# Where the q-k products of chunks 2 to 5 stand among the feed-forward products

## The chip, the cores and the metric

The kernel runs on one core of a Trainium2 chip. The metric is the time of one execution on the device in microseconds (us). Before the change it is 245.2 us, the median of 5 runs (244.85 to 246.48). The engines of a core work side by side, each through its own list of instructions in order: TensorE (PE, matrix products; PEld are its weight loads), VectorE (DVE), ScalarE (ACT), GpSimd (POOL) and SyncE (SP, which here only starts transfers).

## The reference

Two parts follow each other: a retention layer with a running state, and a feed-forward layer on its result.

```python
# q, k, v: 4 batches x 8 heads x 768 positions x 64
for t in range(S):
    state = gamma * state + einsum('bhd,bhe->bhde', k[:, :, t], v[:, :, t])
    y[:, :, t] = scale * einsum('bhd,bhde->bhe', q[:, :, t], state)
# x: y as 3072 rows of 512
xn = x / sqrt(mean(x * x) + 1e-6) * rms_g
out = (silu(xn @ w_gate) * (xn @ w_val)) @ w_out      # 512 -> 1536 -> 512
```

`gamma` is a constant of the head, between 1 - 1/32 and 1 - 1/4096.

## The kernel before, in words

**Chunks and batches.** The 768 positions are cut into 6 chunks of 128 rows (`NCH`, line 35). A chunk holds 4 batches of 128 rows, so 512 rows (`GT`, line 41) go through the feed-forward layer together. Within a chunk the retention is computed as a masked product of q and k, and what came before is added through the state.

**The pieces of one batch of one chunk** (chunks 2 to 5):
- `cast` (line 186): POOL turns q and k into bfloat16 and multiplies v by its decay; SP then starts a transposing transfer each for q and k (line 200), which gives `qT` and `kT`.
- `piece_a` (line 222), "A": 8 products of k and q on PE, 64 rows deep, one for each head, into two PSUM tiles `a_ps0` and `a_ps1` (line 228). DVE multiplies each of them by the causal mask into `am`, two instructions of 128x512 (line 234).
- `piece_y` (line 237), "Y": 8 products `am` by v (line 246), 4 products of q by the state (line 251), and, except in the last chunk, 4 products of k and v for the new state (line 257). DVE then scales the result into `x` (line 261), ACT squares and sums it (`xsq`, line 265), POOL makes `ms` (line 286) and `rstd` (line 289) of the sum, DVE adds the new state to `st_f` (line 273), and POOL casts it to `st_b` (line 282).
- `piece_n` (line 292), "N": DVE multiplies `x` by `rstd` and by `g_bc`, the norm's weights (line 297), and SP starts the transposing transfer that puts the batch's columns into `xnT` (line 299), the input of the feed-forward products of that chunk. `g_bc` is loaded once, by SP (line 456).
- `piece_x` (line 304) does no work for these chunks: it drops the batch's entry from a table.

The four batches share a PSUM pool of 4 tiles for `a_ps`, `y_ps` and `kv_ps` (`aps`, line 49). An A takes two of them, a Y two (one in the last chunk).

**The feed-forward layer of one chunk** is a list of 16 slots (`ffn`, line 337). Slots 0 to 11 ("gv") make one block of 128 hidden units each: 4 products for the gate, 4 for the value (line 351), a SiLU of the gate on ACT (`sg`, line 354), and on DVE the product of `sg` and the value (`hT`, line 355). Slots 12 to 15 ("down") make the output of one batch each: 12 products, the n-th of which needs block n of `hT` (line 386), a copy by ACT (`o_sb`, line 391) and a transfer out by SP (line 392). The gate, value and output products take their PSUM tiles from a second pool of 4 (`fps`, line 50).

**The order of the work** is written out by hand: the kernel runs under a manual schedule (line 31), and what a slot issues stands on each engine in the order in which it was issued. The main loop (line 426) goes through the slots of chunk c's feed-forward layer and, after each slot, issues those pieces of chunk c + 1 that a plan assigns to that slot. A plan gives for each piece four slot numbers, one per batch (`PLAN` for chunks 2 to 5, `PLAN1` for chunk 1; lines 320 and 322). Within one slot the pieces come batch by batch, and within a batch in the order cast, t, a, y, n, x (line 328). In slot 13 the pieces come ahead of the slot's own products (line 433). The loads of q, k and v of chunk c + 2 are issued by SP in the slots 5, 7, 9 and 11, ahead of the pieces of those slots (line 444).

In what follows, **pass c** is the stretch from the first gate product of chunk c to the first of chunk c + 1. The passes 1 to 4 carry the pieces of the chunks 2 to 5, so these four hold all that `PLAN` orders. Pass 0 follows `PLAN1`, and pass 5 has no pieces.

Of the kernel before, what the change touches and what calls it, by code (L numbers as in the profile page):

```python
# [17 lines left out]
def kernel(  # L18
# [297 lines left out]
    def begin(c):  # L316
        cur[c, "xnT"] = work.tile([128, KS, GT], BF16, name="xnT", bufs=2)


    PLAN = dict(cast=(0, 1, 2, 3), t=(1, 3, 5, 7), a=(4, 6, 8, 10), y=(6, 8, 10, 12), n=(8, 10, 12, 13), x=(8, 10, 12, 14))  # L320

    PLAN1 = dict(cast=(4, 6, 8, 11), t=(8, 10, 12, 15), a=(9, 11, 14, 17), y=(10, 13, 16, 19), n=(12, 15, 18, 21), x=(13, 17, 20, 22))

    def attention(c):
        s = [[] for _ in range(24 if c == 1 else 16)]
        s[0].append(lambda: begin(c))
        plan = PLAN1 if c == 1 else PLAN
        pieces = dict(cast=cast, t=piece_t, a=piece_a, y=piece_y, n=piece_n, x=piece_x)
# [156 lines left out]
```

## Time and profile before

| | before |
|---|---|
| median of 5 runs | 245.2 us |
| the profiled execution: its own time | 244.82 us |
| span of its trace, first to last instruction | 243.1 us |
| PE busy | 223.2 us (92%) |
| DVE busy | 128.9 us (53%) |
| POOL busy | 96.2 us (40%) |
| ACT busy | 86.4 us (36%) |
| share of the chain that ended last | PE 79%, DMA 7%, DVE 5%, POOL 3% |

How to read it: a profile is one execution of the program, recorded instruction by instruction. The busy times show how much each engine did, but not what bounded the time. For that there is a chain, followed back from the last instruction: at each step to the instruction that released it, or to the one before it on its engine. A row of the timeline gives the start, the duration, the engine, the line, the tile written and the tiles read, how many instructions are merged in the row, and in brackets the idle time before it and who ended it. Matrix products are pipelined: each is recorded as 0.38 us long, but in a full stream one starts 0.216 us after the other. Likewise DVE instructions recorded as 0.68 us start 0.60 us apart.

### The profile page before, as it was taken

To read this page: it belongs to the slowest core of one execution; us is meant where nothing else is said; L and a number is where in the kernel's file an instruction comes from. 1 tells how busy PE (TensorE), PEld (TensorE's weight loads), DVE (VectorE), ACT (ScalarE), POOL (GpSimd) and SP (SyncE) were. 2 spreads that over 40 slices of the span, in tenths; PEclk is the share of its full clock that TensorE was granted. 3 is DMA by queue.
4 is the path that set the end of the run, shared out by engine and by line. 5 is a ranking of instruction groups with operands and counts; after the bars stand their busy time and mean duration, and the time that the engine had idled before them with its cause. 6 is when DMAs were issued, how large, how long until landed. Compare 5 with 4: busy or idle time off the path is not lost.

```text
span 243.1 us, 4161 instructions
## 1 busy us (share of the span) xinstructions
PE 223.2 (92%) x1534; PEld 115.8 (48%) x1559; DVE 128.9 (53%) x214; ACT 86.4 (36%) x164; POOL 96.2 (40%) x178
## 2 busy tenths in 40 slices
PE   1779999999599989899999999999999999999993
PEld 0546744465245545344555445555445454444443
DVE  6587435777237596035896046895137772234300
ACT  7463334533232243132243222333233433233221
POOL 8977245674733235930224940244920211000000
PEclk9998999999999999999999999999999999999999
DMA  8999999989999799954999454999553114200022
GB/s 137 176 193 206 205 223 199 185 121 226 203 175 276 159 197 211 259 122 96 231 183 198 127 128 80 212 219 199 162 101 65 22 24 115 102 0 3 0 86 88
DMA packets 107157, 35.94 MB, mean 148 GB/s; under 512 B 99008, under 2 KB 103872, under 8 KB 107136
## 3 DMA queue, kind: packets, MB, share of 16 engines
q1 hardware_dynamic: 95232, 29.24, 59.5%
q0 software_dynamic: 11232, 6.29, 19.1%
q8 instruction: 12, 0.20, 0.4%
q10 hardware_dynamic: 672, 0.13, 0.3%
q14 instruction: 9, 0.07, 0.1%
HBM read 28.58 MB, written 6.29 MB: 143 GB/s over the span
## 4 chain that ended last, share of the span: by engine, by line
PE 79%; DMA 7%; DVE 5%; POOL 3%; issue 2%; ACT 1%; SPq 0%; DVEq 0%; POOLq 0%; ACTq 0%
PE g_ps L351 24%; PE v_ps L351 24%; PE o_ps L386 21%; DMA v_f<-in_v_dram 5%; PE a_ps L228 2%; PE y_ps L246 2%; DMA g_bc<-in_moe_rms_g_dram 2%; DVE am L234 2%; PE y_ps L251 1%; PE kv_ps L257 1%; DVE xn L301 1%; PE o_ps L376 1%; PE xt_ps L311 1%; POOL qb L78 1%; DVE x L261 1%
## 5 line engine op out<-in xcount | busy, mean ns | idle before, releaser
L355 DVE TENSOR_TENSOR hT<-sg,v_ps 128x512 bf16<-128x512 bf16 (+1 forms) x73 | 49.5, 679 | 79.4 <-PE v_ps L351 75.0
L351 PE MATMUL g_ps<-xnT,wg_b 128*128 128x512 bf16 (+2 forms) x294 | 73.3, 368 | 1.8 <-ACT o_sb L391 1.1
L351 PE MATMUL v_ps<-xnT,wv_b 128*128 128x512 bf16 (+2 forms) x296 | 73.2, 367 | 0.4
L354 ACT ACTIVATE sg<-g_ps 128x512 bf16<-128x512 f32 (+1 forms) x73 | 42.8, 588 | 61.3 <-PE g_ps L351 59.6
L386 PE MATMUL o_ps<-wo_b,hT 128*128 128x512 bf16 x269 | 61.7, 379 | 0.4 <-issue 0.2
L351 PEld LDWEIGHTS <-wv_b 128*128 128x128 bf16 x304 | 29.1, 98 | 33.1
L351 PEld LDWEIGHTS <-wg_b 128*128 128x128 bf16 x304 | 27.4, 98 | 32.1 <-DMA xnT<-xn 1.5
L386 PEld LDWEIGHTS <-hT 128*128 128x128 bf16 x276 | 26.3, 98 | 29.6
L286 POOL TENSOR_SCALAR ms<-ssq 128x1 f32<-128x1 f32 x24 | 4.5, 189 | 80.5 <-ACT xsq L265 80.1
L391 ACT COPY o_sb<-o_ps 128x512 f32<-128x512 f32 x23 | 13.4, 584 | 39.5 <-PE o_ps L386 37.5
L265 ACT ACTIVATE xsq<-x 128x512 f32<-128x512 f32 x20 | 12.6, 630 | 38.3 <-DVE x L261 38.3
L234 DVE TENSOR_TENSOR am<-a_ps,causal 128x512 bf16<-128x512 f32 x40 | 25.6, 682 | 0.0
L193 POOL TENSOR_TENSOR vp<-v_f,vdec 128x512 bf16<-128x512 f32 x20 | 20.7, 1037 | 2.8 <-DMA v_f<-in_v_dram 2.8
L191 POOL CAST qb<-q_f 128x512 bf16<-128x512 f32 x20 | 12.1, 607 | 14.1 <-DMA q_f<-in_q_dram 13.8
L282 POOL CAST st_b<-st_f 64x256 bf16<-64x256 f32 x40 | 17.1, 427 | 1.3
L297 DVE SCALAR_TENSOR_TENSOR xn<-x,rstd,g_bc 128x512 bf16<-128x512 f32 x16 | 12.6, 788 | 7.2 <-POOL rstd L289 5.6
L261 DVE TENSOR_TENSOR x<-y_ps,ydec 128x512 f32<-128x512 f32 x20 | 13.7, 686 | 3.5 <-PE y_ps L251 3.5
L192 POOL CAST kb<-k_f 128x512 bf16<-128x512 f32 x20 | 12.2, 609 | 5.3 <-DMA k_f<-in_k_dram 5.3
L289 POOL TENSOR_TENSOR rstd<-ms,mhalf 128x1 f32<-128x1 f32 x24 | 13.2, 551 | 2.0
L246 PE MATMUL y_ps<-vp,am 128*128 128x64 bf16 x192 | 10.9, 199 | 2.5 <-DVE am L234 2.4
L246 PEld LDWEIGHTS <-am 128*128 128x128 bf16 x192 | 9.3, 102 | 8.1 <-DVE am L234 3.7
L273 DVE TENSOR_TENSOR st_f<-st_f,kv_ps 128x512 f32<-128x512 f32 x16 | 10.8, 678 | 0.0
(68 smaller groups left out, 134.6 us busy)
## 6 DMA issues: line engine op xcount, KB each, us to landing
out_dram<-o_sb SPq DMA_DIRECT2D x23, 256.0 KB, 2.2
q_f<-in_q_dram SPq DMA_DIRECT2D x21, 256.0 KB, 4.6
k_f<-in_k_dram SPq DMA_DIRECT2D x21, 256.0 KB, 5.1
v_f<-in_v_dram SPq DMA_DIRECT2D x21, 256.0 KB, 5.0
wo_b<-in_moe_w_out_dram POOLq DMA_DIRECT2D x3, 512.0 KB, 5.9
v_f<-in_v_dram POOLq DMA_DIRECT2D x3, 256.0 KB, 5.4
wg_b<-in_moe_w_gate_dram POOLq DMA_DIRECT2D x2, 384.0 KB, 7.6
wv_b<-in_moe_w_val_dram POOLq DMA_DIRECT2D x2, 384.0 KB, 8.5
```

The costliest lines, as they stand in the source:

```text
L193: nc.gpsimd.tensor_tensor(out=vp, in0=v_f, in1=vdec[:, c, :, None].to_broadcast([128, H, D]), op=ALU.mult)
L234: nc.vector.tensor_tensor(out=am[:, i], in0=a_ps[i], in1=mask, op=ALU.mult)
L246: nc.tensor.matmul(y_ps[:, h, :], d["am"][:, i, hp, :], d["vp"][:, h, :], start=first, stop=last, skip_group_check=True)
L261: nc.vector.tensor_tensor(out=x, in0=y_ps, in1=ydec[:, c, :, None].to_broadcast([128, H, D]), op=ALU.mult)
L265: nc.scalar.activation(xsq, x.rearrange("p h d -> p (h d)"), AF.Square, accum_out=ssq)
L282: nc.gpsimd.tensor_copy(st_b[b][r, :, i * 64:i * 64 + 64], st_f[b][r, :, i * 64:i * 64 + 64])
L289: nc.gpsimd.tensor_tensor(out=rstd, in0=ms, in1=mhalf, op=ALU.pow)
L351: nc.tensor.matmul(ps[:, n - n0, :], w_b[:, s, n * 128:(n + 1) * 128], xnT[:, s, t], start=s == 0, stop=s == KS - 1)
L354: nc.scalar.activation(sg, g_ps, AF.Silu)
L355: nc.vector.tensor_tensor(out=hT[:, n0:n1, t], in0=sg, in1=v_ps, op=ALU.mult)
L386: nc.tensor.matmul(o_ps, hT[:, n, b * C:(b + 1) * C], wo_b[:, n, :], start=n == 0, stop=n == NFF - 1)
L391: nc.scalar.copy(o_sb, o_ps)
```

## The change

One line changes, the plan for the chunks 2 to 5. The four numbers are the slots of the batches 0 to 3.

```diff
-    PLAN = dict(cast=(0, 1, 2, 3), t=(1, 3, 5, 7), a=(4, 6, 8, 10), y=(6, 8, 10, 12), n=(8, 10, 12, 13), x=(8, 10, 12, 14))
+    PLAN = dict(cast=(0, 1, 2, 3), t=(1, 3, 5, 7), a=(6, 6, 10, 10), y=(8, 9, 12, 12), n=(10, 11, 13, 13), x=(10, 11, 13, 14))
```

The same in a table (A0 is `piece_a` of batch 0, and so on; the pieces stand in the order of issue):

| slot | pieces before | pieces after |
|---|---|---|
| 4 | A0 | |
| 6 | Y0 A1 | A0 A1 |
| 8 | N0 Y1 A2 | Y0 |
| 9 | | Y1 |
| 10 | N1 Y2 A3 | N0 A2 A3 |
| 11 | | N1 |
| 12 | N2 Y3 | Y2 Y3 |
| 13 | N3 | N2 N3 |

No instruction is added or taken away. The casts, the loads, the feed-forward slots, the pools and the numbers of their buffers stay as they are.

## The prediction

> **What bounds the kernel now.** I read the page's engine line and chain first, then the stretches of the five passes, then PE's waits, and last the timelines around one pair of pieces.
>
> The chain of the page is mostly PE. The stretches (start:end; length, then busy time and instruction count of PE, PEld, DVE, ACT, POOL; clock; DMA share; GB/s) are the passes 1 to 4:
>
> ```profile
> PE 79%; DMA 7%; DVE 5%; POOL 3%; issue 2%; ACT 1%; SPq 0%; DVEq 0%; POOLq 0%; ACTq 0%
> ```
> ```profile
> 64.48:102.44 37.96, 35.81 (x237) 17.58 (x241) 20.61 (x32) 12.53 (x25) 17.36 (x32) 1.00 1.02 208
> 102.44:137.98 35.54, 35.33 (x237) 17.63 (x241) 20.59 (x32) 11.47 (x23) 13.54 (x27) 1.00 0.82 171
> 137.98:173.53 35.55, 35.34 (x238) 17.63 (x241) 20.60 (x32) 12.05 (x24) 14.78 (x29) 1.00 0.89 164
> 173.53:208.18 34.65, 34.44 (x222) 16.76 (x224) 18.27 (x28) 12.05 (x24) 7.39 (x15) 1.00 0.32 77
> ```
>
> Passes 2 to 4 are a full PE stream: 144 products of 0.2157 us (31.06), four A at 0.45 and four Y at 0.67 (both measured below) make 35.54, the length of pass 2. Pass 1 holds the same work and takes 2.42 us more. Its waits name two transfers:
>
> ```profile
> DVE xn L297 <- DMA g_bc<-in_moe_rms_g_dram: 1.6, 1, 1.6
> PEld L351 <- DMA xnT<-xn: 1.5, 1, 1.5
> PE g_ps L351 <- ACT o_sb L391: 1.1, 1, 1.1
> PE y_ps L246 <- DVE am L234: 0.8, 2, 0.4
> ```
>
> The first held N0 of chunk 2, and DVE behind it, until 84.1; Y2 then waited 0.8 us. The second, with PE's 1.1, is the end of the pass: PE waits at 102.4 for the last transposed rows (`o_sb` is named, but weight loads name the transfer).
>
> **Term 1: a mode change on PE is saved.** A row of the timeline: start, duration, instruction, [idle before].
>
> ```profile
> 110.20 1.03 PE L351 MATMUL v_ps<-xnT,wv_b 128*128 128x512 bf16 x4
> 111.16 0.40 PE L228 MATMUL a_ps<-qT,kT 64*128 64x128 bf16 x8
> 111.49 1.04 PE L351 MATMUL g_ps<-xnT,wg_b 128*128 128x512 bf16 x4
> 112.37 1.03 PE L351 MATMUL v_ps<-xnT,wv_b 128*128 128x512 bf16 x4
> ```
>
> The four v products start 0.216 apart, so the next could start at 111.06. A starts at 111.16. Its 8 products run in four pairs 0.057 apart, 0.23 in all, so g could start at 111.39; it starts at 111.49, and its group takes 0.88 where others take 0.863. So an A is 0.23 of products and 0.22 around them, 0.45 together. Two A back to back pay the 0.22 once: 0.67 for 0.90. Two merges a pass: **-0.44 us a pass**. From below, a merge can save nothing, if the second A starts as late as the first; from above 0.22. I take 0.22, since no row shows idle time between products of one shape. A Y fits between other products at no such price: v at 114.09 plus 0.863 is 114.95, Y starts at 114.96; it takes 0.67 (8 products in 0.23, 4 in 0.22, 4 in 0.22) or 0.45 without the state.
>
> **Term 2: DVE's queue ahead of the last `hT`.** Before, one A's two masks (1.20 us at 0.60 spacing) stand ahead of the last `hT`. After, slot 10 puts N0 and four masks there, and down(0) needs that `hT` for its twelfth product. Lags from pass 4 of before:
>
> ```profile
> 196.88 1.28 DVE L234 TENSOR_TENSOR am<-a_ps,causal 128x512 bf16<-128x512 f32 x2
> 198.32 0.69 DVE L355 TENSOR_TENSOR hT<-sg,v_ps 128x512 bf16<-128x512 bf16 x1 [0.16 <-ACT sg L354]
> ```
> ```profile
> 197.08 0.63 ACT L265 ACTIVATE xsq<-x 128x512 f32<-128x512 f32 x1 [2.34 <-DVE x L261]
> 197.71 0.58 ACT L354 ACTIVATE sg<-g_ps 128x512 bf16<-128x512 f32 x1
> ```
>
> The reader is to see that xsq stands ahead of sg on ACT, and that `hT` waits for sg: `hT` starts 0.61 after sg, sg 0.63 after xsq, xsq 0.79 after x (x at 196.28). N takes 0.66, `hT` starts 0.27 after its v stream ends, x 0.66 after its Y starts.
>
> Passes 2 and 3, clock zero at Y0 in slot 8. PE: g9 0.67, Y1 2.40, g10 3.07, v10 ends 4.79, A2 A3, g11 5.46, v11 ends 7.19, twelfth product of down(0) eleven spacings on, 9.56. DVE: hT8 0.27, x0 0.87, xsq0 1.66, sg9 2.29, hT9 2.90, x1 3.50, the state 4.10; xsq1 4.29, sg10 4.92, hT10 5.53; N0 6.13, masks 6.79 to 9.19, hT11 9.19 to 9.88. PE resumed 0.06 after the mask it waited for (masks from 86.00 for 1.28, Y at 87.34). So the product starts at 9.94: **+0.38 us a pass**. Before, the last `hT` of pass 2 (128.03 to 128.71) met a need at 129.3: covered.
>
> Pass 4 has no new state, so each Y is 0.22 shorter on PE and the twelfth product is wanted at 9.12. DVE's chain has the same 9.88, since it hangs on ACT: **+0.82 us**.
>
> [...]
>
> **Term 3: pass 1.** N0 moves from slot 8 to 10, to about 87, after `g_bc` lands at 84.0, so that wait goes (1.34 us, the 2.42 less the 1.08 at the end). What is late next is the end of the pass. SP there:
>
> ```profile
> 94.70 0.58 SPq L64 DMA_DIRECT2D k_f<-in_k_dram  x1
> 95.33 0.95 SPq L64 DMA_DIRECT2D v_f<-in_v_dram  x1
> 96.41 1.12 SPq L392 DMA_DIRECT2D out_dram<-o_sb  x1
> 97.63 2.91 SPq L299 DMA_TRANSPOSE xnT<-xn  x2
> ```
>
> SP has no gap over 0.2 us from 80.0 to 97.6, and the DMA share there is around 1. N2 and N3 were ready at 92.9 and 96.8; their transfers began at 97.6 and 99.3, and the last landed 3.0 later, 102.3. The change puts the same transfers in this queue (N0 one group of loads later, N1 too); on my clock, whose zero is 80.7 here, N3 ends about 96.5. So I keep 102.44: **0 us**, and PE waits 2.5 instead of 1.1. Bounds: if the queue does not bind, the pass ends at 99.97, -2.47; if it grows by one transfer's SP time, +1.2.
>
> **Term 4: the end of passes 2 to 4.** Down(0) ends at 10.16, Y2 and Y3 fill to 11.50, three downs (7.77) to 19.27. DVE: x2 10.82, state 11.42, x3 12.02, state 12.62. POOL: ms 1.60 after x2, 12.42; its rstd and cast hold it to 14.05, then ms of batch 3; N3 0.85 later, 14.90 to 15.76; transfer at 15.85. Before, the last transfers of passes 2, 3 and 4 landed 2.4, 2.5 and 2.4 after their issue, 1.8 or more ahead of need. Now 18.25 against 19.11 (0.16 to spare, as landing to product in pass 1): still 0.86 ahead. **0 us**; if they take 4.2, as the third did in pass 3, 0.94 each in passes 2 and 3. Pass 4 has idle DMA engines (share 0.32). Elsewhere the cover is thin but holds: slot 6's masks end 0.8 us before Y0, and the state of batch 1 leaves the PSUM tile that A3 takes over 0.3 us before A3's use; where DVE is later than that, PE waits for it one to one.
>
> **Sum.** Passes 2 and 3: 2 x (-0.44 + 0.38) = -0.12; pass 4: -0.44 + 0.82 = +0.38; pass 1: 0. Together +0.26: the profiled execution's 244.82 becomes 245.1, and the median, 0.4 above it, 245.2 becomes 245.5.
>
> **Rivals.**
> - *Faster, 243.0 (0.13).* SP's queue in pass 1 does not bind, and pass 1 gives 2.47: 245.5 - 2.5. For it: PE and DVE there are 1.3 us earlier. Against: no gap in SP.
> - *Slower, 247.4 (0.22).* The transposed rows of batch 3 come late in passes 2 and 3: 2 x 0.94 more. It decides when the landing exceeds 3.26 us. For it: N1, an output and N2 now crowd ahead of N3, and 3.6 and 4.2 were seen. Against: the last landed quickly three times.
> - *The merge does nothing, 246.8 (0.08).* Each A still pays its 0.22: 3 x 0.44 more. Against it: same shape, no idle within an A.
> - *Forecast, 245.5 (0.57)*, with its own range 244.7 to 246.3 (the three `hT` waits, 1.58 together, half as long or half as long again).
>
> The range is 243.5 to 247.4: it leaves out most of the fast rival and the tail of the slow ones. About 0.5% (1.2 us) is what a measurement here can tell from no change. Faster by more: 0.13; slower by more: 0.30 (both slow rivals); within: 0.57.
>
> **What would show it.** Right: A rows of x16 taking 0.67 from v to g; two DVE waits of about 0.4 and one of 0.8 ahead of down(0)'s last product; no `g_bc` wait, but a wait of about 2.5 for `xnT` at the end of pass 1. Wrong: pass 1 shorter than 37 us, or waits for `xnT` in passes 2 and 3.

## The result

The changed kernel takes 246.8 us (median of 44 runs) against 245.5 us (median of 79 runs of the kernel before, beside it). The ratio is 1.0044, 95% interval 1.0031 to 1.0058, or 0.8 to 1.4 us more. (The ratio is formed from the undisturbed runs alone, so it is not the quotient of the two medians.) The forecast was +0.26 us, with a range of 243.5 to 247.4: the sign and the range hold, and the loss by the ratio, 1.1 us, is four times as large as the sum.

The profiled execution took 246.86 us, with a span of 245.1. Of the 2.0 us that its span is longer, 1.5 lie ahead of anything that changed: pass 1 starts at 66.02 instead of 64.48. PE's last wait of pass 0, before and after, shows that 0.91 of them were there by its end:

```profile
63.30 0.40 PE L311 MATMUL xt_ps<-ident,xn 128*128 128x128 bf16 x4 [2.65 <-DVE xn L301]
64.21 0.40 PE L311 MATMUL xt_ps<-ident,xn 128*128 128x128 bf16 x4 [2.54 <-DVE xn L301]
```

The other 0.6 came in a stretch at a granted clock of 0.50, from 64.4 to 67.8 (0.57 on average from 64 to 68), which also covers the first 1.8 us of pass 1. Spans of single executions therefore don't compare here. Lengths of passes do, where the clock was full. The chain of the page, and the stretches of the passes 1 to 4 (columns as before):

```profile
PE 64%; DMA 11%; DVE 7%; POOL 7%; SPq 5%; issue 4%; ACT 1%; POOLq 0%; DVEq 0%; ACTq 0%
```
```profile
66.02:103.90 37.88, 36.00 (x237) 17.64 (x241) 20.77 (x32) 12.75 (x25) 16.22 (x29) 0.97 0.98 203
103.90:139.39 35.49, 35.08 (x237) 17.45 (x241) 20.77 (x32) 11.59 (x23) 14.07 (x28) 1.00 0.85 169
139.39:175.08 35.69, 35.25 (x238) 17.39 (x241) 20.78 (x32) 12.17 (x24) 15.67 (x30) 1.00 0.90 165
175.08:210.11 35.03, 34.18 (x220) 16.58 (x225) 18.17 (x28) 12.17 (x24) 9.14 (x16) 1.00 0.33 77
```

Against before, the passes differ by -0.08, -0.05, +0.14 and +0.38 us. The sum had 0, -0.06, -0.06 and +0.38.

**The merge** is there. From PE's timeline in pass 2:

```profile
115.12 1.03 PE L352 MATMUL v_ps<-xnT,wv_b 128*128 128x512 bf16 x4
116.08 0.62 PE L228 MATMUL a_ps<-qT,kT 64*128 64x128 bf16 x16
116.63 1.04 PE L352 MATMUL g_ps<-xnT,wg_b 128*128 128x512 bf16 x3
```

A full stream would go on at 115.98. The 16 products and the time lost around them end at 116.63, and 0.02 follows in the next group: 0.67 for two A, where two A apart cost 0.90.

**The wait for the last `hT`** is there too. DVE, then PE, at the end of slot 10 in pass 2:

```profile
126.23 0.75 DVE L297 SCALAR_TENSOR_TENSOR xn<-x,rstd,g_bc 128x512 bf16<-128x512 f32 x1
126.91 2.47 DVE L234 TENSOR_TENSOR am<-a_ps,causal 128x512 bf16<-128x512 f32 x4
129.30 0.67 DVE L356 TENSOR_TENSOR hT<-sg,v_ps 128x512 bf16<-128x512 bf16 x1
```
```profile
127.29 2.54 PE L387 MATMUL o_ps<-wo_b,hT 128*128 128x512 bf16 x11
130.03 0.39 PE L387 MATMUL o_ps<-wo_b,hT 128*128 128x512 bf16 x1 [0.20 <-DVE hT L356]
```

The twelfth product could start eleven spacings after the first, at 129.66, and starts at 130.03. The loss is 0.37 us. The bracket says 0.20 only, because a product is recorded as 0.38 us long though the next could start after 0.216. Pass 4:

```profile
198.03 2.54 PE L387 MATMUL o_ps<-wo_b,hT 128*128 128x512 bf16 x11
201.20 0.39 PE L387 MATMUL o_ps<-wo_b,hT 128*128 128x512 bf16 x1 [0.64 <-DVE hT L356]
```

Here 200.40 was possible: a loss of 0.80.

**Pass 1** no longer shows a wait for `g_bc`. SP's queue near its end (the last row is the second of the two transfers above it, by itself), and PE's first row of pass 2:

```profile
99.08 0.49 SPq L393 DMA_DIRECT2D out_dram<-o_sb  x1
99.68 2.90 SPq L299 DMA_TRANSPOSE xnT<-xn  x2
101.39 1.19 SPq L299 DMA_TRANSPOSE xnT<-xn  x1
```
```profile
103.90 1.02 PE L352 MATMUL g_ps<-xnT,wg_b 128*128 128x512 bf16 x4 [1.24 <-ACT o_sb L392]
```

From the issue of `g_bc` (81.47) to this row are 22.43 us. Before it was 22.41 (80.03 to 102.44). That the two agree so closely is partly luck: the last transfer was issued 19.92 us after `g_bc` (101.39) instead of 19.32 (99.35), and landed in 2.4 us instead of 3.0.

PE's wait at this place was to be 2.5 us. The row shows 1.24, or 1.40 counted from the time at which the next product could have started. The half clock at the start of the pass (1.8 us of it) had delayed PE by about 0.9, an estimate, and shortened the wait by as much.

### The profile page after: what moved, and what is told of

The parts are those of the page before. It is cut to its first block, busy times and chain, and to the rows that moved or that the text cites. A ratio compares the mean times of both kernels' runs of the same rounds, so it can differ in the third digit from the quotient of the medians.

```text
span 245.1 us, 4152 instructions
## 1 busy us (share of the span) xinstructions
PE 224.2 (91%) x1534; PEld 116.1 (47%) x1559; DVE 129.4 (53%) x214; ACT 86.8 (35%) x164; POOL 98.8 (40%) x178
## 4 chain that ended last, share of the span: by engine, by line
PE 64%; DMA 11%; DVE 7%; POOL 7%; SPq 5%; issue 4%; ACT 1%; POOLq 0%; DVEq 0%; ACTq 0%
PE g_ps L352 19%; PE v_ps L352 19%; PE o_ps L387 18%; DMA v_f<-in_v_dram 7%; SPq L64 5%; DMA wv_b<-in_moe_w_val_dram 4%; DVE am L234 3%; PE a_ps L228 2%; DVE hT L356 2%; PE y_ps L246 1%; PE y_ps L251 1%; DVE xn L297 1%; PE kv_ps L257 1%; POOL qb L78 1%; POOL v_f L83 1%
## 5 line engine op out<-in xcount | busy, mean ns | idle before, releaser
L387 PE MATMUL o_ps<-wo_b,hT 128*128 128x512 bf16 x269 | 63.0, 383 | 1.7 <-DVE hT L356 1.2
L352 PEld LDWEIGHTS <-wg_b 128*128 128x128 bf16 x304 | 28.0, 98 | 32.1 <-issue 3.5
L286 POOL TENSOR_SCALAR ms<-ssq 128x1 f32<-128x1 f32 x24 | 5.1, 212 | 80.0 <-ACT xsq L265 79.2
L234 DVE TENSOR_TENSOR am<-a_ps,causal 128x512 bf16<-128x512 f32 x40 | 24.9, 680 | 0.0
L282 POOL CAST st_b<-st_f 64x256 bf16<-64x256 f32 x40 | 19.2, 480 | 1.3
```

What stands on the lines that cost most here:

```text
L234: nc.vector.tensor_tensor(out=am[:, i], in0=a_ps[i], in1=mask, op=ALU.mult)
L282: nc.gpsimd.tensor_copy(st_b[b][r, :, i * 64:i * 64 + 64], st_f[b][r, :, i * 64:i * 64 + 64])
L352: nc.tensor.matmul(ps[:, n - n0, :], w_b[:, s, n * 128:(n + 1) * 128], xnT[:, s, t], start=s == 0, stop=s == KS - 1)
L387: nc.tensor.matmul(o_ps, hT[:, n, b * C:(b + 1) * C], wo_b[:, n, :], start=n == 0, stop=n == NFF - 1)
```

## The experiments

Each experiment is timed against the kernel before on the same chip. A mean clock is that of one whole execution. Theory S, and Q which grew from it, is the account of the prediction; the rivals stand in the expectations.

**e1 and e2: the new plan in one part only**

```diff
+    OLD = dict(... the plan before ...)
-        plan = PLAN1 if c == 1 else PLAN
+        plan = PLAN1 if c == 1 else PLAN if c == 2 else OLD     # e1
+        plan = PLAN1 if c == 1 else OLD if c == 2 else PLAN     # e2
```

> The new plan for chunk 2 alone (pass 1), the old one for chunks 3 to 5. Theory S (the sum of the prediction: what is lost is the wait for the last hT, above all in pass 4): pass 1 keeps its length of 37.9 us, since its end hangs on SP's queue (22.4 us from the issue of g_bc to the first gate product of pass 2); no g_bc wait; passes 2 to 4 take 35.54, 35.55 and 34.65; time within 0.3 us of the kernel before. Rival R (the loss that the sum doesn't name, about 0.6 us of the 1.1 measured, sits in pass 1): pass 1 is longer by about 0.6 us and the time 0.5 to 0.8 above the kernel before.

> The old plan for chunk 2, the new one for chunks 3 to 5. Theory S: passes 2, 3 and 4 take 35.49, 35.5 to 35.7 and 35.03 us, three waits for the last hT of 0.2, 0.2 and 0.64 us at PE; time 0.3 to 0.5 us above the kernel before. Rival R: the same, but then the new plan in pass 1 must carry the other 0.6 us. If this kernel alone is 1.1 us slower, both are wrong and the loss comes after pass 1 in a way that the trace of one execution does not show.

e1: ratio 1.0035 (1.0010 to 1.0060), +0.86 us. Its one trace has a full clock throughout and a pass 1 of 37.45 us, 22.21 from `g_bc` to pass 2, with PE waiting 1.78 at the end; passes 2 to 4 are 35.55, 35.55 and 34.65. e2: ratio 1.0028 (1.0008 to 1.0048), +0.69 us; passes 1 to 4 are 37.92, 35.49, 35.68 and 35.03.

So the parts that follow pass 1 lose what the sum says (0.46 in the lengths of e2's passes, inside the interval of the time). But the new plan in pass 1 loses as much again, and theory S had put 0 there. By the times R is right about the place (0.86 and 0.69 together are more than the changed kernel's 1.1, but within the intervals). The longer pass 1 that R names is not in the trace of e1, which is of its fastest execution (244.87 us), so the loss is not in every execution. The two executions of e1 at full clock take 245.2 us on average, and the 17 of the kernel before beside it 245.0: too few to say more than that the loss may go with the clock.

**e3 and e4: less on DVE ahead of the last `hT`**

```diff
-    a=(6, 6, 10, 10), ... n=(10, 11, 13, 13), x=(10, 11, 13, 14)
+    a=(6, 6, 10, 10), ... n=(11, 11, 13, 13), x=(11, 11, 13, 14)     # e3
+    a=(6, 6, 11, 11), ... n=(10, 12, 13, 13), x=(10, 12, 13, 14)     # e4
```

> The changed plan with one number different: the norm of batch 0 in slot 11 instead of 10, so that 0.66 us of DVE work goes from ahead of the last hT to behind it. Theory S (the last hT is late by DVE's queue alone): the waits for hT vanish in passes 2 and 3 (35.1 us each) and shrink to about 0.16 us in pass 4 (34.4 us); time 1.2 to 1.4 us below the changed kernel, 0 to 0.8 below the kernel before. Rival W (the wait only moves: the norm and its transfer are then late, and the end of the pass waits for xnT): the hT waits go, but passes 2 and 3 stay at 35.5 us with a PE wait for xnT at their end.

> The changed plan with the second pair of A in slot 11 instead of 10, behind the last gate and value products, and the norm of batch 1 in slot 12. The last hT has then only the norm of batch 0 ahead of it. Theory S: no wait for hT; passes 2 and 3 take 35.1 us, pass 4 34.2; the masks end 0.1 us after batch 3's Y could start, so a wait of 0.1 us or none there; time 1.5 us below the changed kernel and 0.4 to 1.2 below the kernel before. Rival W: the masks now delay Y2 and Y3 by 0.5 us or more, or xnT is late at the end of the pass; passes stay at 35.5 us.

The time of e3 is 1.0051 (1.0019 to 1.0083) of the kernel before, that of e4 1.0031 (1.0001 to 1.0061): no gain where theory S wanted 0 to 1.2 us. The passes of e3:

```profile
64.89:103.41 38.52, 35.03 (x237) 17.48 (x242) 20.69 (x32) 12.75 (x25) 18.47 (x33) 1.00 0.96 201
103.41:140.21 36.80, 36.59 (x237) 17.94 (x241) 20.67 (x32) 11.58 (x23) 11.85 (x25) 0.95 0.82 162
140.21:175.64 35.43, 35.07 (x237) 17.48 (x240) 20.66 (x32) 12.28 (x25) 15.43 (x30) 1.00 0.89 166
175.64:210.01 34.37, 34.16 (x220) 16.58 (x225) 18.07 (x28) 12.06 (x24) 9.03 (x16) 1.00 0.33 76
```

Pass 4 is 34.37, 0.66 below the changed kernel's, as expected: one norm, 0.66 us, went out of the way. Pass 3 gains 0.26 of the 0.38. Pass 2 is 1.3 longer, and its granted clock is 0.95. Its start, and the clock there:

```profile
103.41 1.24 PE L352 MATMUL g_ps<-xnT,wg_b 128*128 128x512 bf16 x4 [3.22 <-issue]
104.44 1.91 PE L352 MATMUL v_ps<-xnT,wv_b 128*128 128x512 bf16 x4
```
```profile
103.00:107.00 4.00, 3.59 (x10) 1.31 (x11) 0.54 (x1) 0.60 (x1) 2.96 (x4) 0.63 0.89 262
```

PE had waited 3.22 us for the last rows of `xnT`, and then four products took 1.7 us (104.44 to 106.15) where they take 0.86. This costs 36.80 - 35.1 = 1.7 us. e4, whose passes 2 to 4 are 35.12, 35.31 and 34.34, 1.0 us below the kernel before together, has a pass 1 of 38.31, whose first 3.3 us (65.60 to 68.9) ran at half clock: the mean granted clock from 65 to 70 is 0.66. The wait for `hT` is settled: it is DVE's queue, and it can be taken away. That the time didn't follow points to pass 1 again.

**e5, e6 and e8: pass 1 without the queue of loads**

```diff
-            if 0 < c < NCH - 2 and i in (5, 7, 9, 11):
-                load(c + 2, (i - 5) // 2)
+            LS = (5, 7, 13, 14) if c == 1 else (5, 7, 9, 11)
+            if 0 < c < NCH - 2 and i in LS:
+                load(c + 2, LS.index(i))
```

e5 is the changed kernel with this edit, e6 the kernel before with it, e8 the kernel e4 with it.

> The changed kernel, but pass 1 issues the loads for batches 2 and 3 of chunk 3 after slots 13 and 14 instead of 9 and 11, behind the last transposing transfers. Theory Q (SP's queue of loads sets the end of pass 1 and gives PE a wait of 1.2 to 3.2 us there; in part of the executions the granted clock then falls to half for one stretch of 3.4 us, which is the loss beyond the schedule's own 0.3 to 0.5): the wait at the end of pass 1 goes, pass 1 takes 35.3 to 35.9 us, fewer executions have a mean clock of 0.993 or less; time 2 to 3 us below the changed kernel. Rival V (the queue is not what binds: the waits come from N2 and N3 themselves, late by DVE): pass 1 stays within 0.5 us of 37.9, and the time within 0.5 of the changed kernel.

> The kernel before with the same two loads moved. Theory Q: its wait at the end of pass 1 (1.1 us) goes too, but the wait for g_bc stays, so pass 1 takes 36.5 to 37.0 us and the time falls by 0.8 to 1.5 us: less than for the changed kernel, since there the wait was longer. Rival V: no change within 0.4 us.

> The second pair of A in slot 11, norm of batch 1 in slot 12, and the two loads moved: no wait for the last hT and none at the end of pass 1. Theory Q: passes 1 to 4 take 35.1 to 35.6, 35.1, 35.1 to 35.3 and 34.3 us, and the time is 2.5 to 3.5 us below the kernel before. Rival V: pass 1 stays at 37.9 and the time 0 to 0.8 below the kernel before.

e5 shows what sets the end of pass 1, and loses the gain: pass 1 falls from 37.88 to 35.51 us, and pass 2 rises from 35.49 to 39.06. The waits of PE in pass 2 of e5:

```profile
114.42 0.40 PE L228 MATMUL a_ps<-qT,kT 64*128 64x128 bf16 x8 [1.53 <-DMA kT<-kb]
139.37 1.02 PE L352 MATMUL g_ps<-xnT,wg_b 128*128 128x512 bf16 x4 [1.70 <-DMA xnT<-xn]
```

SP issues the loads and the transposing transfers one after the other. Moved behind the last `xnT` of pass 1 (the last two from 95.26 to 98.51), the six loads (99.18 to 105.74) stand ahead of the first two `kT` of pass 2 (109.31 and 111.93), and A1 waits 1.53 us for the second; and the end of pass 2 has the wait that pass 1 had (1.70). So SP's queue sets the end of pass 1 (V falls), but passes 1 and 2 together get 1.2 us longer: 74.6 against 73.4 us. In e8 the two take 35.13 and 38.33, 73.5 together. The times are 1.0054 (1.0022 to 1.0085) for e5, 1.0059 (1.0028 to 1.0091) for e6 and 1.0011 (0.9982 to 1.0041) for e8; all three expected gains are missed, and e6's pass 1 (39.60 in its trace, with Y2 waiting for its masks) can't be read for its end: N0 still waited for `g_bc`, and the trace is of e6's longest execution (249.33 us), with a stretch at half clock, in which four products take 1.68 us (90.69 to 92.37) instead of 0.86.

**e7 and e12: PE kept busy in its wait**

```diff
+            if c == 1 and i == 15:
+                fill = aps.tile([128, 256], F32, name="fill", tag="at")
+                for _ in range(14):                              # e12: 9
+                    nc.tensor.matmul(fill, ident, wo_b[:, 0, 0:256], start=True, stop=True)
```

e7 is the changed kernel with this edit, e12 is e9 (below) with it.

> The changed kernel with 14 added products of 128x256 between the last product of pass 1 and the first of pass 2, about 1.5 us of PE work whose result is not used, where PE waits anyway. Theory Q: the schedule stays (pass 1 38 us, ends with SP's queue), but PE's wait there shrinks by 1.5 us, so the half-clock stretch at the start of pass 2 becomes rarer and the mean time falls by 0.3 to 0.8 us, to 0.3 to 0.6 above the kernel before. Rival K (the clock has nothing to do with that wait): the clocks are as in the changed kernel (some 6 in 10 executions at 0.993) and the time is that of the changed kernel or longer.

> e9 with 9 added products of 128x256 in PE's wait at the end of pass 1, about 1.0 us, whose result is not used. Theory Q: passes as in e9, PE's wait there 0.2 us or less; where executions of e9 show a mean clock of 0.993 or less, fewer of these do, and the mean time is 0 to 0.5 us below that of e9. Rival K: clocks and times as in e9, or longer by the added products.

e7: 1.0027 (0.9996 to 1.0058), nominally 0.4 us better than the changed kernel, but not clear. In its trace the 14 products end just as the pass does, and the pass is 0.7 us longer from `g_bc` on (23.14), so they cost something themselves. e12: 0.9962 (0.9933 to 0.9991), 0.5 better than e9, not clear either. The clocks, as executions with a mean clock of 0.993 or less:

| kernels | at 0.993 or less |
|---|---|
| new plan in pass 1, wait left (changed, e1, e3, e4) | 37 of 44, 10, 11 and 12 of 12 |
| new plan in pass 1, wait moved or filled (e5, e8, e7) | 6, 7 and 4 of 12 |
| old plan in pass 1 (before; e2, e9, e10, e11) | 62 of 105; 8, 7, 6 and 7 of 12 |
| old plan, loads moved (e6) | 7 of 12 |
| old plan, wait filled (e12) | 9 of 12 |

One stretch of 3.4 us at half clock makes the mean 0.993 (the changed kernel's trace has one, and that mean). The first two rows are what theory Q wants, but the mean doesn't say where the stretch lay. The 14 traces do. They hold eleven such stretches: three at about 17 to 20 us (before, e7, e12), six at the end of pass 0, behind a wait of PE of 2.1 to 2.7 us (changed, e2, e4, e7, e9, e12), one inside pass 1 (e6), and only one behind PE's wait at the end of pass 1 (e3). Both stretches of e12's trace lie outside the filled wait, so its row says little about filling.

The time does go with the clock. In the changed kernel, its four longest executions left out, the 34 at 0.993 or less take 246.9 us on average and the six at 0.999 or more 245.7. In the three sets of the kernel before beside the experiments (the two longest of one set left out) the two groups differ by 0.1 to 0.6. So the new plan in pass 1 goes with more half-clock stretches, and e3 shows one behind the wait that costs 1.7 us. That the longer wait causes them, and that they make up the whole loss in pass 1, is argued, not shown.

**e9, e10 and e11: the parts that pay**

e9 has the old plan in pass 1 and that of e4 behind it. e10 is the kernel before with `g_bc` loaded earlier. e11 is both.

```diff
-        plan = PLAN1 if c == 1 else PLAN
+        plan = PLAN1 if c == 1 else OLD if c == 2 else PLAN      # e9, e11; PLAN as in e4
```
```diff
             if c == 0 and i == 12:                               # e10, e11
+                nc.sync.dma_start(out=g_bc, in_=moe_rms_g.partition_broadcast(128))
                 load(2, 0, after=landed["wo", 1])
...
                 cast(2, 3)
-                nc.sync.dma_start(out=g_bc, in_=moe_rms_g.partition_broadcast(128))
```

> The old plan in pass 1, and in passes 2 to 4 the pairs of A with the second pair in slot 11 and the norm of batch 1 in slot 12. Theory Q (the merges are worth 0.44 us a pass wherever masks do not stand ahead of the last hT; what the new plan loses in pass 1 comes from SP's queue there and from a longer wait of PE): pass 1 takes 37.9 us with 22.4 from g_bc to the next pass, passes 2 to 4 35.1, 35.1 to 35.3 and 34.3; time 0.7 to 1.1 us below the kernel before. Rival K2 (the longer runs do not come from pass 1 but from PE running denser later): passes 2 to 4 as said, but the time not below the kernel before.

> The kernel before, with the load of g_bc issued in pass 0, ahead of the loads of chunk 2. N0 of pass 1 then never waits for it, and SP's queue of pass 1 is one transfer shorter. Theory Q: the wait for g_bc (1.34 us of PE) was not worth its length, since pass 1 ends with SP's queue; pass 1 gets shorter by that one transfer alone, 0.4 to 1.0 us, with a longer wait at its end, and the time falls by as much or less. Rival V (the wait counts in full): pass 1 falls by 1.3 us or more, to 36.6 at most, and the time by 1.3.

> e9 and e10 together. Theory Q: passes 2 to 4 of e9 and pass 1 of e10; time 1.1 to 2.0 us below the kernel before, if the load of g_bc costs pass 0 nothing. Rival V: 2.2 us below or more.

e9: 0.9981 (0.9949 to 1.0013), -0.5 us, passes 37.60, 35.11, 35.46 and 34.34. The passes are as both expected; the time alone excludes neither Q nor K2. It differs from e4 in pass 1's plan alone, and e4 was 0.8 above the kernel before: the new plan in pass 1 costs about 1.2 by this pair (two chips), 0.86 by e1. e10: 0.9966 (0.9942 to 0.9991), -0.8 us; pass 1 falls by 1.24 to 36.72, with a wait of 1.00 left at its end. That is more than Q's 0.4 to 1.0 and less than V's 1.3, so how much of it was the wait for `g_bc` and how much the queue stays open: both got shorter at once. In pass 0 a new wait of 2.1 us for `wo_b` shows up, and the wait for `xn` falls from 2.65 to 0.69. Pass 0 gives part of the gain back: pass 1 starts at 65.89 in e10's trace and at 65.81 in e11's, but at 64.48 to 65.33 in the six other traces without half clock at the end of pass 0. That is why the time gains less than the pass, as far as single traces can say. e11 is the fastest kernel of the study: 0.9928 (0.9895 to 0.9961), 1.8 us below the kernel before. Its passes:

```profile
65.81:102.67 36.86, 35.46 (x237) 17.59 (x242) 20.60 (x32) 12.64 (x25) 17.41 (x33) 1.00 1.04 208
102.67:137.78 35.11, 34.90 (x236) 17.55 (x241) 20.70 (x32) 11.59 (x23) 12.78 (x25) 1.00 0.88 165
137.78:173.09 35.31, 35.07 (x237) 17.44 (x240) 20.70 (x32) 12.17 (x24) 15.67 (x30) 1.00 0.88 167
173.09:207.43 34.34, 34.12 (x220) 16.70 (x225) 18.09 (x28) 12.09 (x24) 9.17 (x16) 1.00 0.36 75
```

Passes 2 and 4, at 35.11 and 34.34, are within 0.01 and 0.13 of what the prediction's term 1 makes of them with no wait at all (35.54 - 0.44 and 34.65 - 0.44).

## Why the prediction was right, and where it was not

The terms 1 and 2, which it had worked out from rows, were right to a few hundredths. The total is within the range for another reason: the range was wide. The measured median, 246.8 us, lies above the forecast's own 244.7 to 246.3 and is the value given to the rival "the merge does nothing", which the rows refute.

- *Term 1, two A in one group.* 0.67 for them, as said. What the prediction calls a mode change is, in the rows, 0.22 us lost where products of 64*128 stand among those of 128*128. In e9 and e11, without the wait for `hT`, pass 2 is 0.43 shorter than before (0.44 said). The rival "the merge does nothing" is out.
- *Term 2, DVE's queue.* 0.37 and 0.80 measured for 0.38 and 0.82. e3 undoes it by moving one norm on DVE, e4 by moving the second pair behind the last `hT`. This is why the change brings no gain after pass 1: the 0.22 us saved by each pair are paid back by a norm and the masks, which now stand four in a row (2.47 us) ahead of the last `hT`.
- *Term 3, pass 1: the step that failed.* "So I keep 102.44: 0 us" holds for the transfers in the changed kernel's trace (22.43 against 22.41 us, with two differences of 0.6 that cancel), and the fast rival, a shorter pass 1, is out: e5 shows that SP's queue binds. But the step priced the wait of PE at nothing, as if a wait that ends at the same time cost the same. By e1 the new plan in pass 1 costs 0.86 us (0.24 to 1.47), not 0. In single traces the new plan's pass 1 is between 37.45 and 38.52, against 37.60 to 37.96 with the old one (before, e2, e9), so its length alone doesn't show the loss; in e3 PE's wait was followed by 1.7 us lost in pass 2. One trace is too little to call the clock the cause: where the 0.86 us arise stays open. Added to the 0.46 of the passes 2 to 4, 0.86 covers the measured 1.1.
- *The clock after a wait.* After e3's wait of 3.22 us PE ran at a mean granted clock of 0.63 from 103 to 107. At the end of pass 0, six waits of 2.1 to 2.7 us have a stretch at half clock behind them, and six of 2.2 to 2.7 have none: the length of the wait alone doesn't tell them apart, and no run here shows what does.
- *Term 4, the ends of the passes.* 0 was right for passes 2 and 4. Pass 3 ended 0.2 late: its last transfer was issued at 171.90 and landed 3.1 us later, while the products were done at 174.88. Two sizes were off, and neither alone would have used up the 0.86 us in hand. The transfer was issued 0.5 later than said, above all because POOL's cast of the state ahead of batch 3's norm took 1.20 us, not 0.86 (the rows below are of pass 2; before has a cast of 1.20 at 132.65). And it landed in 3.1, not 2.4. The slow rival (1.9 us) did not come, because the last transfers landed in 2.4 and 3.1, not 4.2.

```profile
133.38 1.20 POOL L282 CAST st_b<-st_f 64x256 bf16<-64x256 f32 x2
134.67 0.19 POOL L286 TENSOR_SCALAR ms<-ssq 128x1 f32<-128x1 f32 x1
```

## What to carry to other kernels

Grouping products of one shape saved 0.22 us a pair here, but the instructions that read their results then stood in a group as well (four masks on DVE, 2.47 us): look for what stands behind them in that engine's queue, and put the group where the next urgent result is already through (slot 11 here, not 10). A wait that only moves to the end of a stretch gained nothing here: without the wait for `g_bc`, pass 1 of the changed kernel still took 37.88 us (37.96 before), since it ended with SP's transfers. And in e3 half clock followed a wait of TensorE of 3.22 us and cost 1.7. Before a transfer is moved out of a full queue, add up the stretch behind it too: in e5 the 2.4 us gained in one pass cost 3.6 in the next.

## What the runs showed of the hardware

- A stretch of about 3.4 us at a granted clock of 0.50 began at the end of PE's wait in pass 0, or within 1.1 us of it, in six of the twelve traces in which that wait was 2.1 to 2.7 us (changed 2.54, e2 2.26, e4 2.72, e7 2.52, e9 2.62, e12 2.13). The other six had much the same wait and a full clock (before 2.65, e1 2.25, e3 2.35, e5 2.29, e6 2.50, e8 2.70). e10 and e11, with 0.69 and 0.79, had none there. The wait of 3.22 in e3 was followed by one, the waits of 0.2 to 1.8 us at the ends of passes 1 and 2 by none.
- POOL's two casts of 64x256 took 0.85 us together, but 1.20 where the whole of a norm of DVE ran beside them: in the passes 1 to 3 that is 3 pairs of 12 in the trace of before and 9 of 12 in that of the changed kernel. The norm itself is then mostly recorded as 0.86 instead of 0.74 (0.75 at 126.23). Examples are 132.65 and 132.73 in before, 133.38 and 133.46 in the changed kernel. Beside masks, `hT` or `x` the casts stayed at 0.85 (before, 118.19; changed, 123.33).
